# The first key block loaded in thirds ahead of everything, the sketch matrix loaded to 32 partitions, and a new written-out order

## The chip, the cores and the metric

The kernel runs on one core of a Trainium2 chip. The metric is the device time of one execution in microseconds (us); the median of three runs of the kernel before is 216.59 us, the lowest 216.01 and the highest 217.53. One further execution was recorded by the hardware profiler; all rows of the profile are of that one.

A core has five engines that run side by side, each working through its own list of instructions in order: TensorE (PE in the profile; PEld is its loading of weights), VectorE (DVE), ScalarE (ACT), GpSimd (POOL) and SyncE (SP), which here only issues DMA transfers. ACT and POOL can issue transfers too. An instruction that waits holds up all that stands behind it on its engine.

## The reference

Two blocks follow one another, for 4 batches of 1088 positions, 4 heads of 32 channels:

```python
def phi(x):                                   # r = 8
    a = einsum('rd,bhsd->bhsr', S1, x)
    b = einsum('rd,bhsd->bhsr', S2, x)
    return einsum('bhsi,bhsj->bhsij', a, b).reshape(..., r * r)
q_p, k_p = phi(q), phi(k)
kv  = einsum('bhsf,bhsd->bhfd', k_p, v)
z   = sum(k_p, axis=2)
num = einsum('bhsf,bhfd->bhsd', q_p, kv)
den = einsum('bhsf,bhf->bhs', q_p, z) + 1e-06
x   = num / den                               # -> (batch, 1088, 128)

theta = x @ w_theta
y = w_tok_r @ (x * cos(theta)) + w_tok_i @ (x * sin(theta))
u = x + y
out = u + maximum(u @ w_ch, 0)
```

S1 and S2 and the weights of the second block arrive as 64-bit floats; the kernel reads their words as integers and turns them into 32-bit floats itself.

## The kernel before, in words

Positions are cut into 9 chunks of 128, three chunks to a group, so a batch has three groups (thirds). For each batch the kernel loads k, q and v as tiles of 128 partitions x 1152 floats (`big`, 576 KB each), turns the three groups of k on PE (`kT`, L740) and copies them on ACT (L743), multiplies them with the block matrix of S1 and S2 (`sbk`, built on POOL; `kf`, L340 with `sbk`), forms outer products on DVE (`kp`) and sums them against v on PE.

Beside this, so that the denominator keeps its accuracy, the sums of k are computed in slices. The squares of k are summed per partition (`kq`), a step size is made from the sum on DVE (`key_step`), k is rounded to that step in bf16 (`kb`, DVE, L308 `hf<-big,sm`), the rest is subtracted (`kr`, DVE, L304 `big<-big,hf`), and PE forms Gram matrices of the two: `sums0` (L340 `ps<-hf`) of `kb` alone, then `rest0` (L340 `ps<-big,big`, then `ps<-big`) with `kr`. For batch 0 the squares are shared (`KHALF`): ACT takes 640 of the 1152 columns (L650), DVE the other 512 (L652), and one small DVE addition joins the two.

The sketch matrices are prepared at the very start. `s_t` (S1 and S2 side by side, 32 rows of 16) is loaded by SP four times, once for each head, to all 128 partitions (`read_heads`, L396); `s_2` by ACT (`read_square`, L400). ACT turns the high words (L414), DVE unpacks the low words (L308, L311) and takes the largest value of each row (`m2`, L457), PE turns that (L438, `pt`), DVE makes powers of two of it (`inv`), and ACT and DVE scale and slice S. The weight pair `w_sq` (256 KB) is loaded by SP to `raw` and converted by two ACT instructions (L586, L588) and two DVE instructions (L308, L304 `w`); so is each of the 17 rows of the token weights (1088 KB each), which the second block uses.

The order of all 1018 operations is written out as one list, `ORDER`. An operation is numbered in the sequence in which the program makes it, and each engine issues its operations in the order of the list; waits follow from the tiles that an operation reads and writes. Each `op(...)` carries a duration for the planner that made the list (and `fly`, the time of a transfer in flight); at run time these do nothing. `PLACES` gives each tile its buffer in the pools, so a new list also changes which tile follows which in a buffer. `SPINS` puts small idle matmuls (L381) ahead of an operation, and operation 1 is a longer run of idle matmuls on PE at the start.

Read through the list, the start of each engine's order before is this. SP: s_t, k of batch 0, k of batch 1, w_sq, q of batch 0, k of batch 2, q of batch 1, and then token rows between the others. ACT: load of s_2, a warming sine (L386, before which stands the loading of its table), S high words, S low words, the squares of k, three copies of turned k, the squares of k of batch 1, the first conversion of w_sq; the second stands eleven operations later. DVE: constants, unpacking of S, `m2`, its half of the squares, the addition, `inv` and `key_step` mixed, `kb`, `kr`. PE: idle matmuls, `pt`, two short idle matmuls, the three groups of k and one of batch 1, the powers (L340 `ps<-sm,ones`), `kf` three times, `sums0`, `rest0`. What follows is the same kind of mixture of four batches; from about 100 us on the second block runs, and it ends in products on PE with the rows (`zs`, `big`), whose results are added, multiplied with w_ch, turned and stored.

Of the kernel before, what the change touches and what calls it, by code (L numbers as in the profile page):

```python
# [64 lines left out]
)  # L65
PLACES = (
# [8 lines left out]
)  # L75
SPINS = (
    "70:2 157:2 "
)
WARM = 0
SPLIT = ()  # L80
CHAINS = ((0,), (1,), (2, 3))
QPOOL = (False,) * 4
KEEP = (2, 3)
KEEP_CLS = "big"
# [152 lines left out]
def kernel(  # L237
# [156 lines left out]
    def read_heads():  # L394
        dst = st() if wide else sp()[:, 0]
        SY.dma_start(dst[:, 0:2 * R], bc(s_t.rearrange("d t r -> d (t r)"), 0, [H, D, 2 * R]))  # L396
# [117 lines left out]
    def blocks_t():  # L514
# [7 lines left out]
       lk=1)  # L522
# [881 lines left out]
```

## Time and profile before

| | |
|---|---|
| median of three runs | 216.59 us (216.01 to 217.53) |
| profiled execution | 216.32 us |
| its span, first to last instruction | 214.4 us |
| PE busy | 206.7 us, 96% |
| DVE busy | 181.9 us, 85% |
| ACT busy | 111.2 us, 52% |
| first transpose of k on PE | at 5.55 us |
| transfers | 40.56 MB, mean 189 GB/s |

The profiled execution's own time is 1.9 us above its span. A row of the timeline has the start in us, the time it covers in us, the engine with the line, the operation, the tiles written and read with their shapes, how many instructions were merged, and in brackets the idle time before it and what ended that. SPq and ACTq are the issuing of a transfer by SP or ACT, not the transfer. A row of the stages has first the stage's bounds and length, then the busy time of PE, PEld, DVE, ACT and POOL, the granted clock of PE, the busy share of the 16 DMA engines and their GB/s.

### The profile page before, as it was taken

The page shows a single profiled execution, that of the slowest core. Times are in us where ns is not written, and L with a number is a line of the kernel's source. Part 1 is how long each engine was busy: PE and PEld are TensorE (multiplying, and loading weights), DVE is VectorE, ACT ScalarE, POOL GpSimd, SP SyncE. Part 2 cuts the span into 40 slices and gives each one's busy share as a digit, 9 for nine tenths or more (in the row PEclk, how much of TensorE's full clock was granted, in tenths as well). Part 3 has the DMA queues.
Part 4 walks back from the last instruction along what each step waited for, and adds up shares of the span by engine and source line. Part 5 has one row for each costly group of instructions (what it writes and reads, how often), then busy time and mean ns, then how long its engine had stood idle before and what let it go on. Part 6 is the DMA issues. An engine that isn't in the chain of part 4 may idle for free.

```text
span 214.4 us, 4835 instructions
## 1 busy us (share of the span) xinstructions
PE 206.7 (96%) x1876; PEld 155.1 (72%) x1876; DVE 181.9 (85%) x408; ACT 111.2 (52%) x214; POOL 21.3 (10%) x44
## 2 busy tenths in 40 slices
PE   7999999899999999999999999999989999999993
PEld 4978788779666767666766676578847787888882
DVE  3999999999999999999599819999768999995532
ACT  3999999899999699590720031711229300000000
POOL 2083340200000002000123001010100000000000
PEclk9999999999999999999999999999999999999999
DMA  5999999999894995004456899689974002101113
GB/s 164 419 417 414 417 346 342 380 383 404 302 383 171 354 412 177 2 3 74 76 142 150 120 223 192 125 124 170 241 127 74 14 0 41 28 0 25 28 28 78
DMA packets 52634, 40.56 MB, mean 189 GB/s; under 512 B 45444, under 2 KB 47108, under 8 KB 50436
## 3 DMA queue, kind: packets, MB, share of 16 engines
q1 hardware_dynamic: 35540, 33.71, 48.4%
q0 software_dynamic: 1728, 4.65, 9.8%
q10 hardware_dynamic: 15344, 1.90, 5.9%
q8 instruction: 14, 0.23, 0.4%
q14 instruction: 8, 0.07, 0.1%
HBM read 30.43 MB, written 5.18 MB: 166 GB/s over the span
## 4 chain that ended last, share of the span: by engine, by line
PE 78%; DMA 7%; DVE 7%; issue 4%; ACT 1%; POOL 0%; SPq 0%; DVEq 0%; POOLq 0%
PE ps L340 75%; DMA big<-hf 5%; PE ps L1053 2%; DMA big<-k_l 2%; PE ps L1087 2%; DVE hf L308 1%; DVE g L304 1%; DVE big L304 1%; DVE sm L308 1%; DMA out<-g 1%; DVE sm L311 1%; ACT big L1067 0%; ACT big L650 0%; SPq L396 0%; DVE sm L304 0%
## 5 line engine op out<-in xcount | busy, mean ns | idle before, releaser
L340 PE MATMUL ps<-big,zs 128*128 128x384 f32 (+4 forms) x398 | 109.5, 423 | 0.0
L340 PEld LDWEIGHTS ps<-big,zs 128*128 128x128 f32 x398 | 71.4, 190 | 28.4 <-issue 2.2
L588 ACT ACTIVATE big<-zs 128x1088 int32<-128x1088 uint32 (+1 forms) x18 | 21.4, 1191 | 2.3 <-DVE big L304 2.2
L1191 ACT COPY g<-ps 128x128 f32<-128x128 f32 (+1 forms) x3 | 0.9, 302 | 41.8 <-PE ps L1183 41.5
L304 DVE CUSTOM_DVE_ANT_0 big<-big,big 128x2176 uint16<-128x2176 uint16 x17 | 21.7, 1281 | 0.0
L586 ACT ACTIVATE big<-zs 128x1088 f32<-128x1088 f32 x17 | 20.8, 1232 | 1.8 <-DVE big L304 1.6
L340 PE MATMUL ps<-big,big 128*64 128x64 f32 (+2 forms) x208 | 21.3, 277 | 0.3 <-DMA big<-hf 0.3
L340 PEld LDWEIGHTS ps<-big,big 128*64 128x64 f32 (+1 forms) x208 | 16.5, 154 | 3.9 <-DVE big L304 0.8
L304 DVE TENSOR_TENSOR big<-big,big 128x544 f32<-128x544 f32 x24 | 16.6, 717 | 0.6 <-PE ps L340 0.5
L340 PE MATMUL ps<-mf,big 128*64 128x96 f32 (+1 forms) x108 | 12.8, 268 | 0.0
L308 DVE TENSOR_SCALAR big<-big 128x1088 int32<-128x1088 int32 x17 | 12.3, 726 | 0.5 <-ACT big L586 0.5
L318 POOL DMA_DIRECT2D big<-hf x6 | 6.1, 1018 | 60.8 <-DVE sm L311 39.4
L304 DVE TENSOR_TENSOR g<-lv 128x768 f32<-128x768 f32 x12 | 11.2, 951 | 0.6 <-PE ps L340 0.5
L340 PEld LDWEIGHTS <-hf 128*64 128x64 f16 (+2 forms) x234 | 10.2, 110 | 1.9 <-DVE sm L304 1.4
L991 ACT COPY lv<-ps 128x480 f32<-128x480 f32 x12 | 6.4, 553 | 9.7 <-PE ps L340 9.6
L1100 ACT ACTIVATE g<-ps 128x384 f32<-128x384 f32 x12 | 5.8, 492 | 10.8 <-DMA fq<-g 7.0
L318 POOL DMA_DIRECT2D g<-big x6 | 5.5, 924 | 58.7 <-ACT g L1168 37.5
L340 PEld LDWEIGHTS ps<-w,big 128*128 128x128 f32 x80 | 10.2, 192 | 1.4 <-issue 0.6
L340 PE MATMUL ps<-mv,hf 128*64 128x96 f16 (+1 forms) x162 | 10.8, 207 | 0.2 <-DVE sm L304 0.2
L340 PE MATMUL ps<-w,big 128*128 128x128 f32 x80 | 10.9, 277 | 0.0
L340 PE MATMUL ps<-g,sm 128*64 128x384 f32 x48 | 9.4, 499 | 1.1 <-ACT big L1067 1.0
L304 DVE TENSOR_TENSOR zs<-ps,g 128x768 f32<-128x768 f32 (+2 forms) x15 | 9.4, 627 | 0.8 <-ACT g L1104 0.4
(195 smaller groups left out, 331.8 us busy)
## 6 DMA issues: line engine op xcount, KB each, us to landing
zs<-w_tok SPq DMA_DIRECT2D x17, 1088.0 KB, 12.7
big<-k_l SPq DMA_DIRECT2D x6, 576.0 KB, 6.8
big<-hf POOLq DMA_DIRECT2D x6, 576.0 KB, 10.1
big<-v_l SPq DMA_DIRECT2D x4, 576.0 KB, 14.8
g<-fq SPq DMA_DIRECT2D x6, 384.0 KB, 4.8
big<-q_l SPq DMA_DIRECT2D x3, 576.0 KB, 7.7
fq<-g SPq DMA_DIRECT2D x12, 96.0 KB, 4.6
fq<-g ACTq DMA_DIRECT2D x12, 96.0 KB, 4.5
```

The costliest lines, as they stand in the source:

```text
L304: eng.tensor_tensor(out=o, in0=a, in1=b, op=f)
L308: (eng or V).tensor_scalar(out=o, in0=a, scalar1=s1, scalar2=s2, op0=op0, **kw)
L311: (eng or V).scalar_tensor_tensor(out=o, in0=a, scalar=s, in1=b, op0=op0, op1=op1)
L318: op("G", 0.9, lambda: G.dma_start(dst(), src(), accum_op=ALU.add), w, r, fly=fly)
L340: T.matmul(o, lhs, rhs, start=start, stop=stop, skip_group_check=True)
L586: op("A", 0.22 + n * 0.0009, lambda: A.activation(dfn(), words_of(raw(), n)[1].bitcast(F32), AF.Prelu, scale=2.0**-112, alpha=-(2.0**32)), ...
L588: op("A", 0.22 + n * 0.0009, lambda: A.activation(stp(), words_of(raw(), n)[0].bitcast(U32), AF.Copy, scale=2.0**-29), [stp], [raw])
L991: op("A", act(480), lambda g=g, lp=lp: A.copy(lv().rearrange("p l (c n) -> p l c n", n=HR)[:, :, g * GC:(g + 1) * GC], lp().rearrange("p c ...
L1053: T.transpose(tr()[:, i * P:(i + 1) * P], qp()[:, i * H + 2 * n:i * H + 2 * n + 2].rearrange("p h i j -> p (h i j)"), ident())
L1087: T.transpose(x()[:, i * P:(i + 1) * P], xs()[:, off + i * P:off + (i + 1) * P], ident())
L1100: op("A", act(GW), lambda cs=cs, th=th: A.activation(cs()[:, 0], th(), AF.Copy, bias=ROUND), [(cs, 0)], [th])
L1191: op("A", act(n * P), lambda: A.copy(ot()[:m], ut()[:m]), [ot], [ut])
```

## The change

`SPLIT` now names k of batch 0, so it is loaded by three transfers of one group each, and its squares are three ACT instructions with one sum each in `ka`, which a DVE reduction adds up; DVE's half of the squares and its addition are gone. `read_heads` loads `s_t` once, to partitions 0 to 31, and is issued by ACT instead of SP; the memset of `st` covers the whole tile, and both loads of S wait for it. After unpacking and after `m2`, a new operation `heads` copies the S columns of both words from partitions 0 to 31 to the other three blocks of 32 (three DVE copies). `ORDER`, `PLACES` and `SPINS` are new throughout.

The program makes four operations more, so the numbers shift: 0 to 11 stay, `heads` is 12, old 12 to 43 are one higher, the loads of k of batch 0 are 45, 46, 47, old 45 to 82 are three higher, the squares are 86, 87, 88 with the sum as 89, and old numbers from 86 on are four higher.

```diff
 ORDER = (
-    "6 4 0 2 5 44 1 47 58 3 45 7 48 8 50 11 9 336 10 49 12 29 30 56 84 83 70 13 64 85 71 86 76 14 65 46 128 77 87 15 147 "
-    "51 78 88 72 59 66 73 129 341 89 148 16 90 74 94 17 140 351 130 61 67 141 149 21 95 18 208 25 40 22 53 68 91 23 26 "
...
+    "47 4 0 2 5 61 1 6 46 45 3 50 48 53 88 51 7 62 52 79 8 63 340 87 64 11 345 65 13 9 86 59 10 73 14 80 67 89 15 74 54 "
+    "90 151 132 12 144 91 30 16 31 68 152 93 17 49 92 75 98 69 27 81 18 94 355 76 145 153 19 70 160 33 95 26 77 22 56 23 "
...
 SPINS = (
-    "70:2 157:2 "
+    "13:2 138:1 114:1 "
 )
-SPLIT = ()
+SPLIT = (("k", 0),)
...
     def read_heads():
         dst = st() if wide else sp()[:, 0]
-        SY.dma_start(dst[:, 0:2 * R], bc(s_t.rearrange("d t r -> d (t r)"), 0, [H, D, 2 * R]))
+        A.dma_start(dst[0:D, 0:2 * R], s_t.rearrange("d t r -> d (t r)"))
...
-        op("V", 0.1, lambda: V.memset(st()[:, 2 * R:].bitcast(F32), 0.0), [(st, 0)], [])
-        op("A", 0.46, read_square, [(st, 0)], [], fly=1.6)
-        op("S", 0.1, read_heads, [(st, 1)], [], fly=1.6)
+        op("V", 0.1, lambda: V.memset(st().bitcast(F32), 0.0), [st], [])
+        op("A", 0.59, read_square, [(st, 0)], [], fly=1.6)
+        op("A", 0.5, read_heads, [(st, 1)], [], fly=1.6)
...
+    def heads():
+        for h in range(1, H):
+            V.tensor_copy(sp()[h * D:(h + 1) * D, :, 0:2 * R], sp()[0:D, :, 0:2 * R])
+
+    op("V", 0.35, heads, [(sp, 0), (sp, 1)], [], lk=3)
```

The code that `SPLIT` switches on was in the program before:

```python
for g in range(NG):                                     # in load()
    c = slice(g * GC, g * GC + GC)
    op("S", 1.46 / NG, lambda c=c: SY.dma_start(t()[:, c], src[b][:, c]), [(t, g)], [])
...
def square(g):                                          # in key_sums()
    c = slice(g * GC * HD, g * GC * HD + GC * HD)
    A.activation(flat(j_())[:, c], kc()[:, c], AF.Square, accum_out=ka()[:, g:g + 1])
...
op("V", 0.2, lambda: V.tensor_reduce(out=kq()[:, kc_:kc_ + 1], in_=ka(), axis=AX.X, op=ALU.add), [(kq, kc_)], [ka])
```

Read through the new list, the orders at the start are these. SP: third group of k (47), w_sq (61), second group (46), first group (45), k of batch 1, q of batch 0, q of batch 1, k of batch 2. ACT: load of s_2 (5), load of s_t (6), warming sine (3), squares of the third group (88), S high words (7), both conversions of w_sq (62, 63), squares of the second group (87), S low words (9), squares of the first (86), two copies of turned k (80, 74), squares of k of batch 1, the third copy. DVE: unpacking of S (8), first step of w_sq (64), `m2` (11), second step of w_sq (65), S low words (10), maximum of `pt` (14), sum of the squares (89), `inv` (15), `key_step` (90), `heads` (12), `kb` (91), the step of batch 1, `kr` (92). PE: idle matmuls, the third group of k, two short idle matmuls, `pt`, the other two groups, two groups of batch 1, the powers (16), `sums0` (93), `kf` three times, `rest0` twice. The end of the list is, by kind, nearly the same as before: the last operations on PE are the nine products of 128 columns, two turns and two products with w_ch.

More of the change, by code (lines that the diff above doesn't have):

```diff
@@ L429 @@
         op("V", 0.2, lambda: V.memset(sp(), 0.0), [sp], [])
-        op("A", 0.46, read_square, [(sp, 0)], [], fly=1.6)
-        op("S", 0.1, read_heads, [(sp, 0)], [], fly=1.6)
+        op("A", 0.59, read_square, [(sp, 0)], [], fly=1.6)
+        op("A", 0.5, read_heads, [(sp, 0)], [], fly=1.6)
     def powers(mfn, m, n, name):
```

82 rows, old and new, of tables (ORDER, PLACES) are left out of this document.

## The prediction

> **What bounds the kernel now.** I read the page's head first, then the stages, then what PE waited for, then the opening by engines.
>
> ```profile
> span 214.4 us, 4835 instructions
> ...
> PE 206.7 (96%) x1876; PEld 155.1 (72%) x1876; DVE 181.9 (85%) x408; ACT 111.2 (52%) x214; POOL 21.3 (10%) x44
> ```
>
> ```profile
> 0.00:5.00 5.00, 3.66 (x8) 2.20 (x9) 2.00 (x27) 1.94 (x4) 1.28 (x9) 1.00 0.48 145
> 5.00:10.00 5.00, 4.91 (x85) 4.22 (x85) 4.33 (x14) 4.28 (x12) 0.26 (x1) 1.00 1.03 419
> 20.00:30.00 10.00, 9.54 (x164) 8.05 (x163) 9.82 (x34) 9.90 (x23) 3.99 (x7) 1.00 1.02 390
> 30.00:40.00 10.00, 9.63 (x240) 8.49 (x239) 9.75 (x25) 9.47 (x20) 0.25 (x1) 1.00 1.05 347
> 40.00:60.00 20.00, 19.39 (x197) 15.24 (x196) 19.44 (x42) 18.99 (x37) 1.24 (x1) 1.00 0.97 373
> 60.00:80.00 20.00, 20.00 (x108) 13.41 (x107) 19.81 (x33) 17.60 (x25) 0.00 (x0) 1.00 0.83 323
> 140.00:160.00 20.00, 18.98 (x87) 13.93 (x86) 16.37 (x28) 4.72 (x10) 1.72 (x2) 1.00 0.95 174
> ```
>
> PE is idle for 214.4 - 206.7 = 7.7 us in all. From 5 us to 60 us PE, DVE, ACT and the transfers are all over 85% busy, most over 95%; past 60 us PE alone is full. Four stages carry nearly all idle time of PE between 20 and 200 us: 0.46 + 0.37 + 0.61 + 1.02 = 2.5 us. So the end is set by PE: when it begins real work, how much there is, and what it waits for in between. The granted clock (the 1.00 ahead of the DMA share) is full throughout.
>
> ```profile
> 1.34 3.57 PE L381 MATMUL ps<-idle 128*128 128x384 f32 x6 [1.34 <-POOL idle L383]
> 4.70 0.42 PE L438 MATMUL ps<-ident,m 128*2 128x128 f32 x1
> 4.91 0.85 PE L381 MATMUL ps<-idle 128*128 128x384 bf16 x2
> 5.55 2.07 PE L740 MATMUL ps<-ident,big 128*128 128x128 f32 x12
> ...
> 8.01 1.27 PE L340 MATMUL ps<-sbk,g 128*64 128x64 f32 x36
> 9.08 0.48 PE L340 MATMUL ps<-hf 128*64 128x64 bf16 x18
> 9.57 1.27 PE L340 MATMUL ps<-big,big 128*64 128x64 f32 x36
> ```
>
> These are PE's first rows: idle matmuls to about 4.7 us, `pt`, two short idle ones, four groups of k, the powers, `kf`, `sums0`, `rest0`. The reader is to see that real work starts at 5.55 us, except `pt`, and runs on almost without a break. The long idle run stands at the head of PE's order in both kernels, so whatever lands early, PE's first real instruction can't start before 4.70.
>
> **The change, part by part.** ACT first, since the squares now go through it.
>
> ```profile
> 0.95 0.60 ACTq L400 DMA_DIRECT2D st<-s  x1
> 1.59 1.28 ACT L386 ACT_TABLE_LOAD   x1 [1.59 <-DVE hm L365]
> 2.88 0.20 ACT L386 ACTIVATE warm<-halfpi 128x1 f32<-128x1 f32 x1
> 3.05 0.25 ACT L414 ACTIVATE sp<-st 128x48 f32<-128x48 f32 x1
> 4.11 0.24 ACT L426 ACTIVATE sp<-sz 128x48 f32<-128x48 int32 x1 [0.81 <-DVE sz L308]
> 5.39 0.74 ACT L650 ACTIVATE big<-big 128x640 f32<-128x640 f32 x1 [1.04 <-DMA big<-k_l]
> 6.04 0.19 ACT L650 ACTIVATION_READ_ACCUMULATOR big<-big 128x1 f32 x1
> 6.43 1.43 ACT L743 COPY g<-ps 128x384 f32<-128x384 f32 x3 [0.21 <-PE ps L740]
> ...
> 8.91 0.45 ACT L586 ACTIVATE w<-zs 128x256 f32<-128x256 f32 x1
> ...
> 13.23 0.43 ACT L588 ACTIVATE big<-zs 128x256 int32<-128x256 uint32 x1
> ```
>
> The table load begins at 1.59, as ACT's issue of s_2 ends (0.95 + 0.60). A second issue on ACT therefore pushes it back. Its price lies between the cheapest and the dearest SP issue of the rows below, 0.45 (two for 0.90) and 0.75; I take 0.52, nearer the first, since the transfer has 32 rows instead of 128. Warm sine ends at 3.08 + 0.52 = 3.60.
>
> Squares of one third: 384 columns take 1.43 / 3 = 0.48 on ACT, and reading the sum adds 0.10 (0.74 alone became 0.84, to 6.23): 0.57. Then in ACT's order: third group to 4.15, S high words 0.25 to 4.40, conversions of w_sq 0.45 + 0.43, overlapping by about 0.1, to 5.20, second group to 5.75, S low words to 5.95, first group to 6.50. Before, ACT was done with its square at 6.23 and DVE had the joined sum at 6.42. So splitting the load buys nothing at this point: all three squares stand in one queue, with w_sq inside it.
>
> Do the transfers arrive in time?
>
> ```profile
> 0.72 0.75 SPq L396 DMA_DIRECT2D st<-s_t  x1
> 1.54 0.90 SPq L616 DMA_DIRECT2D big<-k_l  x2
> ```
>
> ```profile
> 3.00:3.50 0.50, 0.50 (x2) 0.20 (x2) 0.17 (x1) 0.30 (x2) 0.00 (x0) 1.00 0.48 111
> 3.50:4.00 0.50, 0.50 (x2) 0.26 (x1) 0.43 (x5) 0.00 (x0) 0.00 (x0) 1.00 0.91 369
> ```
>
> Issued at 1.54, k moves from about 3.4 (1.86 later), and ACT sees it whole at 5.39. Issued at 0.72, the first third moves from 2.58; at the 419 GB/s of 5 to 10 us a third (192 KB) takes 0.47 and w_sq 0.63. In SP's order: third group moved by 3.05, w_sq by 3.7, second group by 4.15, first by 4.6, each seen some 0.6 later (k before: 3.4 + 1.4 = 4.8, seen at 5.39). Each is there just before ACT asks (3.60, 4.40, 5.10, 5.95). The transfers as a whole start 0.8 us earlier; PE hardly waits for them (below), so I count that at nothing.
>
> DVE next.
>
> ```profile
> 3.99 0.16 DVE L457 TENSOR_REDUCE m<-sp 128x2 f32<-128x16 f32 x1
> ...
> 6.26 0.16 DVE L304 TENSOR_TENSOR sm<-sm,sm 128x1 f32<-128x1 f32 x1
> 6.45 0.57 DVE L308 TENSOR_SCALAR sm<-sm 128x1 int32<-128x1 int32 x4
> 7.13 0.22 DVE L308 TENSOR_SCALAR sm<-ident,sm 2x2 f32<-2x2 f32 x1
> 7.26 0.86 DVE L308 TENSOR_SCALAR hf<-big,sm 128x1152 bf16<-128x1152 f32 x1
> 8.16 1.36 DVE L304 TENSOR_TENSOR big<-big,hf 128x1152 f32<-128x1152 f32 x1
> ...
> 11.35 0.28 DVE L308 TENSOR_SCALAR w<-w 128x256 int32<-128x256 int32 x1
> ...
> 18.24 0.42 DVE L304 CUSTOM_DVE_ANT_0 w<-w,big 128x512 uint16<-128x512 uint16 x1
> ```
>
> The sum of the three columns costs 0.16, as the reduction of L457: 6.66. From the joined sum to `kb` took 7.26 - 6.42 = 0.84 with `inv` and `key_step`: 7.50. `heads` stands between and delays `kb` too: three copies, each between 0.14 (0.57 / 4) and 0.22; I take 0.17, 0.5 in all: `kb` starts at 8.0 instead of 7.26, **0.74 later**. Behind it DVE has less to do, as both w_sq steps (0.28 + 0.42 = 0.70) now lie in the idle time ahead of it. So by about 18 us DVE stands where it stood, within 0.1. ACT has w_sq's 0.88 less behind 6.5 as well, so it is up to 0.8 ahead.
>
> PE then. The third group is turned at 4.70 (0.52 = 2.07 / 4), `pt` waits for `m2`: S high words end at 4.40 instead of 3.30, from there to the end of `m2` took 4.15 - 3.30 = 0.85, and the w_sq shift of 0.28 stands between: 5.5. The two short idle matmuls lie in that wait. Four groups from 5.8 to 7.85, the powers (before, between the end of the groups at 7.62 and `kf` at 8.01) to 8.1; then `sums0` stands ahead of `kf` in the new order and waits for `kb`, 8.0 + 0.86 = 8.86: **a stall of 0.75 on PE**. `sums0` to 9.3, `kf` 1.07 to 10.4; `rest0` needs `kr`, 8.9 + 1.36 = 10.25, no wait. Before, `rest0` began at 9.57, with one group of k (0.5) fewer done: 10.4 - 10.07 = **0.3 us behind**. Idle matmuls further on are two quarters in both lists. The multiplications of the whole program are the same, and POOL's work too, in another order.
>
> What PE waits for later, from the waits:
>
> ```profile
> PE ps L340 <- DMA big<-hf: 0.3, 1, 0.3
> ```
>
> This is the only wait of its matmuls for a transfer. Past the opening the list is new throughout and I can't follow each wait; all that a better order could save between 20 and 200 us is the 2.5 us above, and a worse one adds. I carry it as zero, with both ends in the range. Sum: +0.3. The profiled execution took 216.32, 0.27 below the median of 216.59; I set the forecast against the median: 216.59 + 0.3 = **216.9**.
>
> **The rivals.**
>
> *The opening gains.* If the squares are not late (a cheaper second issue, copies that overlap), `sums0` doesn't stall: 0.75 less than forecast, 216.1; with half of the later idle time (1.2) gone too, by ACT and the transfers being 0.8 ahead, 214.9. For it: ACT and DMA were full from 5 to 60 us. Against it: PE's rows begin at 4.70 at the earliest, and hardly a wait of PE names a transfer. All of it, 2.5 + 0.45, would give 213.6.
>
> *ACT's order waits for what lands late (slower).* Conversions of w_sq and S high words stand ahead of two squares and the copies of turned k. This issue row is the only one of w_sq:
>
> ```profile
> zs<-w_sq SPq DMA_DIRECT2D x1, 256.0 KB, 5.1
> ```
>
> There it stood behind two whole k. Should it land 5.1 after its issue again (about 1.2), at 6.3 instead of 4.3, ACT stands still for 1.9, squares, `kb`, `sums0` and everything on PE behind them move by that: 216.9 + 1.9 = 218.8. It decides once w_sq lands after 4.4, or S after 4.15. S: before, it was there at most 3.05 - 1.47 = 1.6 after its issue ended; from 2.1, that is 3.7. If it queues behind the two transfers ahead of it in time, it moves by up to 0.47 + 0.63 to 4.8, 0.7 late: 217.6. [...]
>
> *The new order stalls PE further on (slower).* DVE is 97% busy from 20 to 80 us (9.82 + 9.75 + 19.44 + 19.81 of 60), ACT as full up to 60, so a planner's wrong duration turns into a PE wait at once. If the stalls of 2.5 double: 216.9 + 2.5 = 219.4.
>
> **How the numbers follow.** The runs before spread by 0.7%, so about 1% (2.2 us) is what can be told from no change. Forecast 0.55, all within 1%. Gaining opening 0.18, of which 0.05 reaches below 214.4. Late landing 0.14, of which 0.05 stays within 1% and 0.09 is slower. Later stalls 0.13, slower. Faster 0.05, same 0.73, slower 0.22. The range leaves out the best of the gains and the worst of the stalls: 215.1, the gain but for its last 0.2, to 219.3.
>
> **What would show it.** Right: `kb` (L308 `hf<-big,sm`) starts near 8.0, `sums0` (L340 `ps<-hf`) near 8.9 with PE idle just before it on DVE; the table load starts near 2.1; from 60 us on PE is as full as before, ahead or behind by under 1 us. Wrong: ACT idle before L586 or L414 on a transfer; `sums0` without a wait; or PE idle between 20 and 200 us well off 2.5 us, which is the part I couldn't work out.

## The result and the profile after

The changed kernel takes 218.15 us (median of 7 runs, 216.86 to 220.48); before takes 217.12 us (median of 7 runs on the same chip, 216.01 to 217.53). The ratio is 1.0065, 95% interval 1.0036 to 1.0094: slower by 0.65%, 1.4 us (1.0 us by the medians), which is inside the 1% that was called no change. The forecast was 216.9 against 216.59, slower by 0.14%. That lies below the interval: the direction held and the time is in the range given, but the loss is about 1 us larger than the sum, and it came about in another way. Ratios here and below leave out executions that took over 1.5% longer than the fastest of their kernel (one of seven of the changed kernel, five of twelve of both_undone below, none of the kernel before), medians don't, so the two can differ by some tenths of a per cent.

The head of the page of the changed kernel: span, and busy time, share and count of instructions by engine.

```profile
span 215.4 us, 4829 instructions
...
PE 205.2 (95%) x1876; PEld 155.4 (72%) x1876; DVE 180.4 (84%) x409; ACT 113.2 (53%) x218; POOL 21.9 (10%) x44
```

The span grew by 1.0 us (214.4 to 215.4). PE is idle for 10.2 us instead of 7.7. Its own work counts 1.5 us less; how much of that is fewer idle matmuls and how much the modelled ends, I didn't trace. Where the idle time lies is in the stages of the changed kernel (stretch, its length, then busy time and count of PE, weight loads, DVE, ACT and POOL, the granted clock, the DMA share and GB/s):

```profile
0.00:5.00 5.00, 3.66 (x8) 2.36 (x9) 1.03 (x21) 2.08 (x5) 1.03 (x7) 1.00 0.57 172
5.00:10.00 5.00, 3.33 (x20) 2.11 (x18) 3.86 (x19) 3.93 (x12) 0.91 (x2) 1.00 0.97 336
20.00:30.00 10.00, 9.01 (x198) 7.87 (x194) 9.35 (x36) 9.18 (x22) 3.02 (x5) 1.00 1.03 401
30.00:40.00 10.00, 8.56 (x190) 7.90 (x191) 8.56 (x19) 8.72 (x16) 0.66 (x1) 1.00 1.05 344
40.00:60.00 20.00, 19.20 (x257) 16.11 (x254) 19.81 (x48) 18.72 (x38) 0.85 (x1) 1.00 0.87 341
140.00:160.00 20.00, 20.00 (x87) 14.79 (x87) 15.65 (x25) 5.53 (x12) 1.74 (x2) 1.00 0.89 181
```

Against the rows of before, PE's idle time moved like this:

| stretch, us | idle before | idle after |
|---|---|---|
| 0 to 10 | 1.43 | 3.01 |
| 10 to 20 | 0.20 | 0.58 |
| 20 to 40 | 0.83 | 2.43 |
| 40 to 60 | 0.61 | 0.80 |
| 140 to 160 | 1.02 | 0 |

So there are two losses of 1.6 us, one in the opening and one between 20 and 40 us, two small ones, and one gain of 1.0 us at 140. The opening first, from the timeline of all engines (start, duration, engine and line, operation, and in brackets the idle time before it and what ended that):

```profile
0.98 0.61 ACTq L400 DMA_DIRECT2D st<-s  x1
1.63 0.36 ACTq L396 DMA_DIRECT2D st<-s_t  x1
2.02 1.28 ACT L386 ACT_TABLE_LOAD   x1 [2.02 <-DVE bdm L368]
3.42 0.51 ACT L649 ACTIVATE big<-big 128x384 f32<-128x384 f32 x1
4.91 0.25 ACT L414 ACTIVATE sp<-st 128x48 f32<-128x48 f32 x1 [0.89 <-DMA st<-s_t]
5.06 0.42 ACT L592 ACTIVATE w<-zs 128x256 f32<-128x256 f32 x1
6.74 0.53 ACT L649 ACTIVATE big<-big 128x384 f32<-128x384 f32 x1 [0.30 <-DMA big<-k_l]
8.36 0.54 DVE L462 COPY sp<-sp 32x32 f32<-32x32 f32 x3
8.89 0.88 PE L746 MATMUL ps<-ident,big 128*128 128x128 f32 x6 [1.58 <-DMA big<-k_l]
8.94 0.88 DVE L308 TENSOR_SCALAR hf<-big,sm 128x1152 bf16<-128x1152 f32 x1
10.00 0.47 PE L340 MATMUL ps<-hf 128*64 128x64 bf16 x18
```

The first third is squared at 3.42, but ACT then stands 0.89 us until S is there at 4.91. The last square waits for the last third (6.74), `kb` starts at 8.94, and PE stands 1.58 us for k of batch 1, which lands at 8.87. The DMA view of both kernels from 2 to 9 us shows what was moved. Before:

```profile
DMA packets 787, 2.41 MB, mean 344 GB/s; under 512 B 197, under 2 KB 197, under 8 KB 787
```

and after:

```profile
DMA packets 925, 2.11 MB, mean 301 GB/s; under 512 B 155, under 2 KB 519, under 8 KB 925
issues: line engine op xcount, KB each, median us to landing
...
big<-k_l SPq DMA_DIRECT2D x2, 192.0 KB, 4.1
```

More packets, 519 of them under 2 KB instead of 197, and 0.3 MB less moved in the same 7 us, although the changed kernel starts earlier. The second loss shows in PE's timeline: rows whose idle time ends in "issue", with no semaphore behind them. After:

```profile
24.41 0.33 PE L340 MATMUL ps<-sbk,g 128*64 128x64 f32 x3 [0.84 <-issue]
...
32.55 0.46 PE L340 MATMUL ps<-mf,big 128*128 128x96 f32 x2 [1.25 <-issue]
...
44.90 0.60 PE L1059 MATMUL ps<-ident,g 128*128 128x128 f32 x4 [0.52 <-issue]
```

Before has one of them:

```profile
42.02 0.65 PE L1053 MATMUL ps<-ident,g 128*128 128x128 f32 x4 [0.61 <-issue]
```

### The profile page after: what moved, and what is told of

Same layout as the page of the kernel before. It is cut to its first block, busy times and chain, and to the rows that moved or that the text cites. A ratio compares the mean times of both kernels' runs of the same rounds, so it can differ in the third digit from the quotient of the medians.

```text
span 215.4 us, 4829 instructions
## 1 busy us (share of the span) xinstructions
PE 205.2 (95%) x1876; PEld 155.4 (72%) x1876; DVE 180.4 (84%) x409; ACT 113.2 (53%) x218; POOL 21.9 (10%) x44
## 4 chain that ended last, share of the span: by engine, by line
PE 84%; DVE 8%; DMA 3%; issue 2%; ACT 1%; SPq 1%
PE ps L340 79%; DMA big<-k_l 3%; PE ps L1059 2%; PE ps L1093 1%; DVE lv L304 1%; DVE big L304 1%; DVE g L304 1%; DVE sm L304 1%; PE ps L746 1%; DVE hf L308 1%; ACT big L663 1%; SPq L611 1%; DVE big L308 1%; PE ps L961 0%; DVE big L311 0%
## 5 line engine op out<-in xcount | busy, mean ns | idle before, releaser
L340 PE MATMUL ps<-big,big 128*64 128x64 f32 (+2 forms) x208 | 20.5, 276 | 0.3 <-DVE big L304 0.3
L318 POOL DMA_DIRECT2D big<-hf x6 | 5.6, 938 | 77.4 <-DVE hf L308 52.9
L1174 ACT COPY g<-ps 128x384 f32<-128x384 f32 (+1 forms) x6 | 2.6, 456 | 19.7 <-PE ps L340 19.7
L304 DVE TENSOR_TENSOR g<-lv 128x768 f32<-128x768 f32 x12 | 11.1, 945 | 0.1
L1073 ACT COPY big<-ps 128x384 f32<-128x384 f32 x12 | 5.7, 483 | 10.3 <-PE ps L340 10.0
L340 PEld LDWEIGHTS ps<-w,big 128*128 128x128 f32 x80 | 10.2, 192 | 0.9
L340 PEld LDWEIGHTS ps<-mf,big 128*64 128x64 f32 (+1 forms) x108 | 9.0, 155 | 1.5 <-issue 1.4
```

The source lines that it names most:

```text
L304: eng.tensor_tensor(out=o, in0=a, in1=b, op=f)
L318: op("G", 0.9, lambda: G.dma_start(dst(), src(), accum_op=ALU.add), w, r, fly=fly)
L340: T.matmul(o, lhs, rhs, start=start, stop=stop, skip_group_check=True)
L1073: op("A", act(GW), lambda g=g, xp=xp: A.copy(xt()[:, g * GW:(g + 1) * GW], xp()), cells(xt, g * GW, (g + 1) * GW), [xp])
L1174: op("A", act(w), lambda: A.copy(u(), yp()[:, :w]), [uT], [yp])
```

## The experiments

My first theory after the result: the opening's transfers cost the time (thirds make the queue slow, and S on ACT's queue lands behind them). The rival: the new list loses it further on, whatever the opening does. The yardstick, beside the time, is how far PE has come: the time by which it has begun the matmul behind its 92nd, 473rd and 727th, read from its counts over stretches that begin at 0. In the changed kernel the last two stand behind the pauses at 32.55 and 44.90. These times are of the one profiled execution of each kernel; in those of s_by_sp, both_undone and k_first_s_act the granted clock was at half for some 3.4 us between 8 and 15 us, in that of s_ahead_again behind 33 us.

| kernel | 92 | 473 | 727 | ratio to before |
|---|---|---|---|---|
| before | 10.1 | 29.5 | 42.1 | 1 |
| after | 12.3 | 32.6 | 45.0 | 1.0065 |
| k_whole | 11.9 | 32.3 | 44.3 | 1.0092 |
| s_by_sp | 14.2 | 32.5 | 44.9 | 1.0037 |
| both_undone | 12.5 | 31.1 | 43.8 | 1.0017 |
| old_opening | 11.1 | 33.1 | 45.7 | 1.0088 |
| s_ahead_again | 11.3 | 32.0 | 45.2 | 1.0023 |
| only_thirds | 11.5 | 30.9 | 42.7 | 1.0066 |
| only_s | 13.1 | 32.6 | 44.5 | 1.0151 |
| k_first_s_act | 14.0 | 33.6 | 45.7 | 1.0169 |

**k_whole: the changed kernel with k of batch 0 in one transfer.** S stays on ACT, squares stay in thirds.

```diff
+LOADS = False
-        if (nm, b) in SPLIT:
+        if (nm, b) in SPLIT and LOADS:
```

> The changed kernel, with k of batch 0 loaded whole again, first on SP, w_sq behind it; squares still by thirds on ACT, S still by ACT. Theory A (the thirds slow the transfers): the rate from 4 to 9 us is back over 400 GB/s, k of batch 1 is there by about 7.2 instead of 8.9, PE's wait of 1.6 us for it goes, and the time falls by 1.0 to 1.6 against the changed kernel, to about 216.5 to 217. Theory B (the late S and the row of squares on ACT are what costs): the first square starts at about 4.6 instead of 3.4, the last ends at about 7 as now, kb stays near 8.9, and the time stays within 0.5 of the changed kernel.

Measured 217.71 us, ratio 1.0092 (1.0053 to 1.0131). The stretch from 4 to 6 us moves at 418 GB/s:

```profile
4.00:6.00 2.00, 1.40 (x8) 0.81 (x6) 0.33 (x2) 1.26 (x5) 0.00 (x0) 1.00 1.05 418
```

The changed kernel has 286 there:

```profile
4.00:6.00 2.00, 2.00 (x8) 1.28 (x6) 0.74 (x5) 1.11 (x5) 0.00 (x0) 1.00 0.87 286
```

PE no longer waits for k of batch 1. But S is there later still, and PE waits for DVE instead, 1.31 us at 6.71 for `m2`, which comes from S, and 1.33 us at `sums0`:

```profile
5.36 0.24 ACT L416 ACTIVATE sp<-st 128x48 f32<-128x48 f32 x1 [0.29 <-DMA st<-s_t]
...
9.93 0.47 PE L342 MATMUL ps<-hf 128*64 128x64 bf16 x18 [1.33 <-DVE sm L310]
```

So the thirds cost transfer rate here (286 against 418 GB/s), and taking them away alone wins nothing: the next wait stands where the first one stood.

**s_by_sp: the changed kernel with S issued first, by SP.** Thirds stay.

```diff
-        A.dma_start(dst[0:D, 0:2 * R], s_t.rearrange("d t r -> d (t r)"))
+        SY.dma_start(dst[0:D, 0:2 * R], s_t.rearrange("d t r -> d (t r)"))
...
-        op("A", 0.5, read_heads, [(st, 1)], [], fly=1.6)
+        op("S", 0.5, read_heads, [(st, 1)], [], fly=1.6)
```

> The changed kernel, with S issued by SP as its very first transfer instead of by ACT (still 32 partitions, still copied on). Theory B: S is there before 3.2 instead of 4.9, ACT does not wait for it, S high words end near 4.2, the last square ends near 6.5, kb starts near 8.0 instead of 8.9, and the time falls by 0.5 to 0.9. Theory A: k of batch 1 is still late (8.9 or later, as everything on SP moves back by 0.4), PE waits for it as long as before, and the time stays within 0.4 of the changed kernel.

Measured 217.48 us, ratio 1.0037 (1.0008 to 1.0065). S is converted at 4.15 without a wait for it. k of batch 1 is the later one now, as the thirds come after one more transfer:

```profile
9.80 1.18 PE L752 MATMUL ps<-ident,big 128*128 128x128 f32 x6 [2.48 <-DMA big<-k_l]
```

PE reaches count 92 1.9 us after the changed kernel, and count 473 at the same time (32.5 and 32.6). A delay of the opening is gone by 33 us. That spoke against my first theory.

**both_undone: k whole and S first by SP,** the two edits above together, S's high words ahead of the squares.

```diff
+        if (nm, b) in SPLIT and LOADS:
...
+        op("S", 0.5, read_heads, [(st, 1)], [], fly=1.6)
 ...
 ACT:  ... [S high], square, w_sq x2, [-S high], square, S low, square ...
```

> The changed kernel, with both repairs at once: k of batch 0 whole, and S issued by SP as the first transfer, its high words turned on ACT ahead of the squares. If the two late landings are two parallel waits that each hold kb and PE to about 9 us, so that removing one alone shows the other: S high words end near 3.3, the squares near 6.2, kb starts near 7.5, sums0 near 8.5, no PE wait over 0.5 in the opening, and the time falls by about 1.2 against the kernel with k whole alone, to within 0.5 of the kernel before. If the new order behind the opening keeps what it loses, PE's pauses without a releaser stay near 24, 32 and 44 us, and the time stays 1 or more above the kernel before.

Measured 217.07 us against 215.77 for the kernel before on that chip, ratio 1.0017 (0.9985 to 1.0048): not to be told from before by the ratio, 1.3 us slower by the medians. My number for the opening was wrong: `kb` came at 9.10 instead of 7.5, as the squares stand behind the whole of k (4.99) and the two conversions of w_sq. The pauses at 24 and 32 us are gone in the profiled execution; one is left, at 43.72, of 0.83. But PE was held back in it by a clock of 0.50 from 12 to 14 us, and s_ahead_w_late (below), with nearly the same list, a clock of 1.00 and count 92 at 11.8, has pauses of 1.22 and 0.90 us at 24.36 and 32.15. So it isn't shown that the two edits took them away.

**old_opening: the program of before with its first 40 places of the list, then the list and buffers of after.**

```diff
-ORDER = (before)
+ORDER = (the first 40 of before, then the rest in the order of after)
```

> The program before, with the first 40 places of its list, and from there on the changed kernel's list and buffers (the conversions of w_sq left where they stood before). If the loss lies in the opening alone, and the new order behind it is as good or better (it has no wait of 1.0 near 158 us), the time is 215.3 to 216.6, at or below the kernel before. If the new order behind the opening loses by itself (the two pauses of PE of 0.8 and 1.25 us at 24 and 32 us), it is 217.3 or more.

Measured 218.56 us, ratio 1.0088 (1.0064 to 1.0112). The opening is good (`sums0` at 8.24), and the time is lost behind it, in rows like those above:

```profile
22.04 0.42 PE L341 MATMUL ps<-sbt,sm 64*64 64x64 f32 x8 [0.43 <-issue]
24.87 0.33 PE L341 MATMUL ps<-sbk,g 128*64 128x64 f32 x3 [0.54 <-issue]
33.05 0.46 PE L341 MATMUL ps<-mf,big 128*128 128x96 f32 x2 [1.29 <-issue]
45.68 0.60 PE L1054 MATMUL ps<-ident,g 128*128 128x128 f32 x4 [0.79 <-issue]
```

The first of these stands behind the 311th matmul and is of another kind than those that come by count (below). It isn't a clean half of the change: the moved conversions of w_sq take ACT from 8.80 to 9.56, and PE waits 0.9 us for ACT further on.

**only_thirds: before, with k of batch 0 in three transfers in the same place of its own list.**

```diff
-        if (nm, b) in SPLIT:
+        if (nm, b) in THIRDS:
```

> The kernel before, with one change: k of batch 0 is loaded by three transfers of one third each, in the same place of SP's order. Theory A: the rate from 4 to 9 us falls below 360 GB/s, k of batch 1 comes at 8 or later instead of 7.0, and the time rises by 0.8 to 1.6. Theory B: two more issues of 0.45 on SP move what follows by 0.9 in issue but not in landing, and the time stays within 0.4 of the kernel before.

Measured 217.59 us, ratio 1.0066 (1.0037 to 1.0094), 1.4 us. The rate between 4 and 6 us falls to 201 GB/s:

```profile
4.00:6.00 2.00, 1.89 (x12) 1.24 (x10) 0.45 (x4) 1.19 (x4) 0.51 (x2) 1.00 0.83 201
```

Before has 407 there:

```profile
4.00:6.00 2.00, 2.00 (x9) 1.34 (x8) 0.96 (x4) 0.85 (x2) 0.51 (x2) 1.00 1.01 407
```

PE is 1.4 us late at counts 92 and 473 and 0.6 at 727, and the profiled span is 0.9 us longer (215.3 against 214.4). With the list of before, most of the opening's delay passes on.

**only_s: before, with S by ACT to 32 partitions and copied on.**

```diff
-        SY.dma_start(dst[:, 0:2 * R], bc(s_t.rearrange("d t r -> d (t r)"), 0, [H, D, 2 * R]))
+        A.dma_start(dst[0:D, 0:2 * R], s_t.rearrange("d t r -> d (t r)"))
...
+    op("V", 0.35, heads, [(sp, 0), (sp, 1)], [], lk=3)
```

> The kernel before, with one part of the change: S issued by ACT to 32 partitions and copied on by DVE (k of batch 0 whole, in its place, which is now first on SP). Theory B: S is there at about 4.8, its high words end near 5.0 instead of 3.3, the low words near 6.1, and the square of k, behind both on ACT, starts near 6.2 instead of 5.4; kb starts near 8.2 and the time rises by 0.6 to 1.2. If S late is harmless: within 0.4 of the kernel before.

Measured 219.56 us, ratio 1.0151 (1.0115 to 1.0187): 3.3 us. PE is 3.0 us behind at count 92, and the profiled span is 2.3 us longer (216.7).

```profile
1.61 0.38 ACTq L398 DMA_DIRECT2D st<-s_t  x1
...
6.23 0.24 ACT L416 ACTIVATE sp<-st 128x48 f32<-128x48 f32 x1 [2.72 <-DMA st<-s_t]
```

The issue ends at 1.99 and 4 KB are there at 6.2. The DMA view shows what ACT's queue (q10) moved: nothing up to 3.75 us, s_2 from 3.75 to 4.25, nothing from 4.25 to 5.00, S from 5.00 to 5.75 (packets, MB, share of 16 engines):

```profile
q10 hardware_dynamic: 16, 0.00, 2.6%
...
q10 hardware_dynamic: 48, 0.00, 4.7%
```

SP's queue had moved 0.56 MB by 3.75 us and 1.09 by 5.00, and a load of k is 0.59 MB. So in this run the two queues took turns, and one turn was a whole load: k, s_2, k of batch 1, S. S had two loads of the other queue ahead of it, as s_2 took ACT's first turn.

**k_first_s_act: before, with k first on SP and S, still to 128 partitions, issued by ACT ahead of s_2.**

```diff
-        SY.dma_start(dst[:, 0:2 * R], bc(s_t.rearrange("d t r -> d (t r)"), 0, [H, D, 2 * R]))
+        A.dma_start(dst[:, 0:2 * R], bc(s_t.rearrange("d t r -> d (t r)"), 0, [H, D, 2 * R]))
```

> The kernel before with only the two first transfers changed: k of batch 0, whole, is SP's first, and S goes as before to 128 partitions, but by ACT, ahead of s_2, so that it is issued at the same time as k and not behind it. If it is the place behind queued packets of k that makes S late, S is there by about 3.3, k at about 4.6 instead of 5.4, the squares end 0.8 earlier, PE turns k from 4.7, and the time falls by 0.3 to 0.8 against the kernel before. If S on ACT's queue is late in any case, it comes at 4.5 or later and the time rises by 0.5 or more.

Measured 219.83 us, ratio 1.0169 (1.0138 to 1.0199). The conversion waits until 7.24, and what it waits for last is s_2, which is now the second load on ACT's queue:

```profile
7.24 0.24 ACT L416 ACTIVATE sp<-st 128x48 f32<-128x48 f32 x1 [3.43 <-DMA st<-s]
```

PE is 3.9 us behind at count 92, and by the ratio 3.65 us are lost. S, first on ACT's queue this time, was moved earlier than in only_s though it has 128 rows: of ACT's packets 110 begin from 3.75 to 4.50 us, behind the first k, 21 from 4.50 to 5.65 and 17, with s_2, from 5.65 to 6.75. So in both runs what comes late is the load that goes second on ACT's queue (S at 6.23, s_2 at 7.24); the number of partitions isn't the reason here.

**shifted_count: the changed kernel with 24 idle one-column matmuls ahead of `pt`,** to see whether the pauses belong to an operation or to a count.

```diff
+            if o.i == 13:
+                fill(None, 0)
...
+        if not quarters:
+            for _ in range(24):
+                T.matmul(o[:, :1], idle().bitcast(BF16)[:, 0:P], idle().bitcast(BF16)[:, :1], start=True, stop=True,
+                         skip_group_check=True)
+            return
```

> The changed kernel with 24 matmuls of one column put ahead of pt, where PE waits anyway. If the pauses of PE without a releaser come with the number of matmuls issued (they stood behind the 346th, 473rd and 727th in the changed kernel), they stand behind the same numbers again, so at operations that come 24 matmuls earlier in the program. If they belong to the operations, they stand behind the 370th, 497th and 751st. The time stays within 1 of the changed kernel.

One execution, 225.42 us with a clock of 0.967, so its time isn't used. The pauses stand in front of other operations than in the changed kernel:

```profile
22.86 0.27 PE L343 MATMUL ps<-g,ident 64*64 64x64 f32 x1 [0.78 <-issue]
30.74 0.30 PE L343 MATMUL ps<-g,big 128*32 128x64 f32 x3 [1.60 <-issue]
47.49 0.56 PE L343 MATMUL ps<-sbk,g 128*64 128x64 f32 x11 [2.24 <-issue]
```

By count they are where they were: behind the 347th, 473rd and 728th matmul, 346, 473 and 727 in the others. They belong to the count. Counts 346 and 473 lie 127 matmuls apart, 473 and 727 twice that; 127 matmuls with their 127 weight loads are 254 instructions.

So the next view to read is the DMA view's row of the instruction queue (packets, MB, share of 16 engines). In the changed kernel between 30.00 and 30.75 us:

```profile
q8 instruction: 1, 0.02, 8.1%
```

One packet of 16 KB (the page of the changed kernel has 14 on this queue, 0.23 MB in all), 0.081 x 16 x 0.75 = 1.0 us long. In stretches of 0.25 us, the changed kernel has such packets beginning at 15.75, 22.00, 30.25, 36.25, 42.25, 49.50 and 55.75; before at 13.00, 19.25, 26.75, 33.25, 39.75, 45.75 and 55.00 (each the start of its stretch). The pauses shown of these two kernels end 2.2 to 2.7 us after one of them: 24.41 after 22.00, 32.55 after 30.25, 44.90 after 42.25, and before 42.02 after 39.75. How far PE had come when the packet ahead of count 473 began is in the counts of these four stretches from 0 (each ends where the 0.25 us begin in which the packet begins), of before, after, both_undone and s_ahead_again (a kernel told of below), in this order:

```profile
0.00:26.75 26.75, 24.86 (x448) 20.07 (x448) 22.55 (x92) 22.88 (x55) 9.93 (x30) 1.00 0.93 366
```

```profile
0.00:30.25 30.25, 25.68 (x461) 20.93 (x462) 23.97 (x102) 25.38 (x64) 12.32 (x33) 1.00 0.94 358
```

```profile
0.00:28.50 28.50, 24.33 (x428) 20.59 (x428) 23.04 (x96) 24.19 (x60) 10.87 (x32) 0.94 0.94 367
```

```profile
0.00:29.50 29.50, 26.23 (x468) 21.71 (x468) 24.96 (x106) 25.74 (x64) 12.37 (x33) 1.00 0.94 365
```

At 448 and 428 PE had 25 and 45 matmuls left to count 473, and there is no pause. At 461 and 468 it had 12 and 5, and stands 1.25 and 1.82 us, until 2.30 and 2.41 us after the start of the packet's stretch. Two kernels lie between: s_by_sp, at 454, stands 0.39 us, and k_whole, at 457, 0.90. That such a packet brings PE's next instructions is my reading of the queue's name, of these counts and of an estimate: the 1876 matmuls and 1876 weight loads of the changed kernel over its 14 packets are 268 to a packet, near the 254 above. No row says what a packet holds. Of the seven packets up to 56 us in the changed kernel three were followed by a pause, of those in the kernel before one.

**s_ahead: both_undone with ACT converting all of S ahead of the squares and w_sq behind them, and DVE copying S's heads while k moves.** It takes 1.5 us out of the opening and leaves the rest of the new list alone, so it asks directly whether an earlier opening arrives at the end.

```diff
 ACT:  ... S high, [S low], square, [-w_sq x2], square, square, [w_sq x2], copies ...
 DVE:  ... words of S, [max, S low words, copies of the heads], sum of squares, kb, [w_sq] ...
```

> The kernel of both_undone with the opening put in another order: ScalarE converts all of S ahead of the squares and w_sq behind them, VectorE finishes S and copies its heads while k moves. From both_undone's rows: k there at 4.99, three squares to 7.1, the row sums and two steps 0.6, so kb at 7.7 to 8.0 (there 9.10) and sums0 at 8.6 to 8.9 (there 10.04), 1.1 to 1.4 us earlier. Theory A (with the new list the first 45 us take up a shift of the opening, and the pauses without a releaser behind matmul counts 346, 473 and 727 set what is left): count 854 less than 0.5 us earlier than in both_undone, ratio 0.998 to 1.004. Theory B (the opening passes on to the end, as with the list before): count 854 1.1 us earlier, at 53.8, and ratio 0.995 to 0.997, faster than both kernels.

Measured 216.45 us against 216.51, ratio 0.9957 (0.9925 to 0.9989), which looked like a gain.

**s_ahead_w_late: the same with w_sq behind the square of batch 1.**

```diff
 ACT:  ... square, square, square, [-w_sq x2], copies, square of batch 1, [w_sq x2], copy ...
```

> As s_ahead, with the two conversions of w_sq on ScalarE put behind the square of the second load of k instead of ahead of TensorE's copies. kb and sums0 as in s_ahead; the copies of the transposes 0.85 earlier. Theory A: the same time as s_ahead but for the pauses, ratio 0.998 to 1.004. Theory B: up to 0.5 us below s_ahead, ratio 0.993 to 0.997.

Measured 217.56 us, ratio 1.0015 (0.9980 to 1.0049). No gain.

**s_ahead_again: s_ahead a second time.**

> s_ahead a second time, to see whether its 0.9957 stands and where an execution at full clock has its time. If the gain is real: ratio again 0.993 to 0.999 at full clock, count 92 at 11.3 as in s_ahead, count 854 at or below 54.0, and the wait of 1.0 us for big of ScalarE between 140 and 160 us gone as in the changed kernel. If the first result was chance: 0.999 to 1.004, as both_undone had.

Measured 217.39 us against 215.89, ratio 1.0023 (0.9989 to 1.0057). The gain was chance, or too small for these runs; neither version beats before. Its trace shows where the better opening goes. `sums0` begins at 8.25 instead of 10.04, PE is 1.2 us ahead of both_undone at count 92, and then:

```profile
23.20 0.33 PE L342 MATMUL ps<-sbk,g 128*64 128x64 f32 x3 [0.56 <-issue]
...
31.91 0.46 PE L342 MATMUL ps<-mf,big 128*128 128x96 f32 x2 [1.82 <-issue]
```

The packet for count 473 began at 29.50, 1.0 us after that of both_undone, though PE was ahead; the lead was waited away here. Then the clock halved for about 3 us (next-to-last columns: clock, DMA share, GB/s):

```profile
32.00:34.00 2.00, 2.00 (x24) 1.99 (x25) 1.01 (x2) 0.81 (x2) 0.00 (x0) 0.92 1.02 348
34.00:36.00 2.00, 2.00 (x13) 2.00 (x12) 0.56 (x3) 1.33 (x4) 0.00 (x0) 0.50 1.08 349
36.00:38.00 2.00, 2.00 (x22) 1.81 (x20) 2.00 (x6) 1.36 (x4) 0.00 (x0) 0.73 1.03 323
```

**rows_left_out: s_ahead with three loads of w_tok left out,** to see whether the packet is late because the DMA engines are full.

```diff
+        if few:
+            op("G", 2.2, lambda: G.memset(raw().bitcast(F32), 0.0), [raw], [])
+        else:
             op("S", n * 0.00255, lambda: SY.dma_start(raw(), src), [raw], [])
```

> The kernel of s_ahead with three of the seventeen loads of w_tok (rows 4, 0 and 3, 1088 KB each) left out: GpSimd clears their tiles instead, so these rows of the weights are zero and the time is not that of the whole computation. Some 3.3 MB, 8.4 us at 400 GB/s, are missing from what the DMA queues carry between 10 and 31 us. In every kernel one packet of the instruction queue (16 KB, 1.0 us long) lies 2.2 us ahead of the first matmul after counts 346, 473 and 727; in s_ahead it comes at count 313 for 346 and only at 468 for 473. Theory A (the packet waits its turn behind the data on full DMA engines): with the share of the DMA engines well under 1 between 22 and 30 us the packet for count 473 comes by count 450 and the pause of 1.5 to 1.8 us there is under 0.5. Theory B (the packet is asked for late, and what the queues carry has no part in it): it comes again at 461 to 470 and the pause is 1.2 to 1.9. If the share stays at 1, the run doesn't tell them apart.

One execution, 221.04 us. It didn't tell the two apart: later loads moved up, and the share stayed at 0.87 to 1.08 in every 2 us from 22 to 32. The packet for count 473 began at 31.75 and the pause was 1.71.

## Why the prediction was right and where it was wrong

- **Table load and third.** Forecast 2.1 for the table load, measured 2.02. The first third was there when the warm sine ended (3.42 for the square). Right.
- **S and the squares.** S was forecast at 3.7; it was there at 4.91. My rival's figure, S queuing behind the two transfers ahead of it, was 4.8, and the rival was right in this: S, second on ACT's queue, came at 4.91 behind a third and w_sq (448 KB), at 5.36 behind k and w_sq (832 KB, k_whole) and at 6.23 behind two k (1152 KB, only_s). My 3.7 was 1.6 us after the end of the issue, the wait of before, where S was the first load on SP's queue, and I gave late landings of S and w_sq together only 0.14. Nor had I seen that S would need the second turn, as s_2 had the first (only_s).
- **The transfers "at nothing".** This is the step that failed. I took 419 GB/s, the rate of before, for the thirds and all behind them. They ran at 286 to 323 GB/s from 4 to 9 us, and k of batch 1 came at 8.87 instead of before PE wanted it: 1.58 us of PE's time. The earlier start was there (111 GB/s from 1.75 to 2.00 us, while k of before begins to move between 2.50 and 3.00; my 2.58 and 3.4 were both too late), but the slower rate had used it up by 9 us.
- **`kb` and `sums0`.** Forecast 8.0 and 8.86, measured 8.94 and 10.00, by the two points above. The copies of the heads were 0.5 as forecast (0.54). The opening cost 1.6 us of PE's time, not 0.3. My signs of being wrong came: ACT idle before L414 on a transfer (0.89), `sums0` without a wait, as PE had waited before it for k of batch 1, and 3.2 us of idle time on PE between 20 and 200 us instead of 2.5.
- **The later order "at zero".** The sum of the changes past 10 us was a cancellation, not a zero: 1.6 us more of pauses between 20 and 40 us, 1.0 less at 140 (the wait for ACT's L1067 is gone). The forecast had only waits for engines in mind there; those pauses name no engine and go with the packets of the instruction queue. (DVE is 98% busy from 20 to 80 us, 58.82 of 60, not 97%; nothing hangs on it.)
- **The end.** That 218.15 lies within 1% of 216.9 is partly luck. The opening was 1.3 us too cheap, and the idea of the later stages had neither the pauses nor the stretch where the lag shrinks; the first cost 1.3 us more by count 727, the second gave back 1.9. PE is 2.9 us behind at count 727, and the span is 1.0 us longer. Of the 1.9 between, 1.0 is the wait at 140; the other 0.9 goes between 45 and 140 us, nearly all of it with PE full in both, and which instructions give it back I didn't trace.

What the runs show of the cause: each of the two loading edits costs time by itself (1.4 and 3.3 us in the list of before). With both undone in the changed kernel the ratio shows no loss any more (1.0017), with one undone it still does (1.0092 and 1.0037), as the other's wait is next; by the medians, with the executions that the ratio leaves out, 1.3 us of loss remain with both undone. So how much of the 1.4 us the two edits make up isn't settled. The later pauses go by how far PE is when the instruction packet begins (428 to 468 matmuls of 473), in six kernels. What the runs don't show: why thirds slow the loads behind them up to 9 us (beside their rows there are two more issues on SP, and k of batch 1 is issued at 2.57 us instead of 1.62 in k_whole; the two aren't told apart), why the instruction packet comes when it does, and so whether the new list would be faster if it came earlier.

## What to carry to other kernels

Issue a small load that is wanted first ahead of the large ones: issued first on SP, S was converted at 4.15 without a wait for it (s_by_sp); second on ACT's queue, it held the conversion until 4.91, 5.36 and 6.23 (the changed kernel, k_whole, only_s). In only_s ACT's queue got a turn after each whole load of 576 KB, so what went second there waited for two of them. Cutting a load to have its first piece early cost rate here (201 GB/s against 407 from 4 to 6 us in only_thirds), and the bill came at the next load (1.58 us of PE's time for k of batch 1 in the changed kernel), so price the whole opening at the rate of the cut rows. When a wait on PE has no releaser, count matmuls to it and look for the instruction packet: s_ahead_again, 1.2 us ahead of both_undone at count 92, waited 1.82 us at such a point.

## What was not expected of the hardware

- Packets of 16 KB on the instruction queue, and pauses of PE of 0.2 us (only_thirds) to 2.24 us (shifted_count) that name no engine, behind counts that lie 127 matmuls or twice that apart. With 428 and 448 of 473 matmuls begun when the packet began PE did not stand, with 454 to 468 it stood 0.39 to 1.82 us. In the changed kernel the DMA engines' share was 1.03 to 1.07 in the 2 us around its three pauses; that the full engines make the packet late was asked and stays open.
- After the pause of 1.82 us (s_ahead_again) the granted clock fell to 0.50 in the stretch from 34 to 36 us, with pairs of matmuls of one kind going from 0.43 to 0.71 us. The changed kernel, with pauses of 0.84 and 1.25, kept 1.00. The length of the wait alone doesn't settle it: waits of 1.36 us (both_undone, at `sums0`) and 1.46 (s_ahead, at 31.57) were followed by 0.50 too, the changed kernel's wait of 1.58 at 8.89 was not.
- Loads of 192 KB in rows of 1.5 KB brought the rate from 4 to 6 us to 201 GB/s in only_thirds, against 407 before, and in the changed kernel the whole loads behind them were slow too: 313 GB/s from 6.5 to 9 us, when no such rows were left, against 430 before.
- In only_s two queues took turns by whole loads: a load of 4 KB, issued by 1.99 us, was moved from 5.00 us on, behind two loads of 576 KB of the other queue.
